# Filler matmuls, exponential buffers, halves of the softmax and the order of projection's products in a fused attention and two-MLP kernel

## The chip, the cores and the metric

The kernel runs on one core of a Trainium2 chip. The metric is the device time of one execution in microseconds; the time of a kernel is the median of its runs. TensorE (PE in the profile) multiplies and writes only into PSUM, which has eight banks here of 128 partitions by 512 float32 words; VectorE (DVE), ScalarE (ACT) and GpSimd (POOL) do the elementwise work, and SyncE (SP) issues most of the DMAs.

## The reference

Attention over 32 memory slots, then two MLPs, all in float32. B is 4, H 8, S 576, D 64, M 32; there are 2304 tokens, and the model is 512 wide.

```python
a = softmax(phi, axis=2)                       # over the 576 positions
k_m = einsum('bhsm,bhsd->bhmd', a, k)          # 32 memory rows per head
v_m = einsum('bhsm,bhsd->bhmd', a, v)
attn = softmax(q @ k_m.T / 8, axis=-1)         # over the 32 slots
x = (attn @ v_m) as (2304, 512)
x = ((x @ w_a) * (x @ w_b)) @ w_out            # 512 -> 1536 -> 512
h = x @ w_in                                   # 512 -> 2048
out = (h * sigmoid(1.702 h)) @ w_out2          # 2048 -> 512
```

The weights come as 64-bit floats and are decoded on the chip.

## The kernel before, in words

**The order is planned, not written.** Every piece of work is a Python generator, a stream with a priority, that yields requests: an engine with a cost in ns, a slot of a buffer, or a mark that another stream sets. `Order.run` (line 179) keeps one clock per engine, takes the request with the earliest start (in steps of 40 ns, then by priority, low numbers first) and lets that stream emit its instructions. So the order of the instructions on each engine's in-order queue comes from the planner's costs. A load sets its mark with the time at which it is taken to land, as soon as its DMA is issued in the plan (`load`, line 125; in the front 300 bytes per ns and 2500 ns to land, counted from 2000 ns); a stream that waits for that mark is resumed at once and uses the time as the earliest start of its next request.

**The front.** There are eight attention units, one for each batch and group of four heads: unit n is batch n // 2. `loads` (line 1626) issues the first loads in the order of the tuple `FIRST` (line 48): phi, k and v, and q of a unit, and raw weight pieces, each into a slot of its buffer; a load whose buffer isn't free holds up all behind it, on SyncE's queue too. Six raw buffers exist at first. `memory(n)` (line 524) takes a slot of `et_s`, the buffer of exponentials, then transposes phi on PE (line 551 in units 0 and 1, 548 later), takes maxima on DVE (555, 557), exponentials on ACT (561, 565), transposes back (569, 573), multiplies with k and v (589), and ends with the scores (628), which go transposed into `sT` (635). It holds two PSUM banks of `bank_a` meanwhile. `queries(n)` (499) transposes q (508). `softmax` (647) then runs over `sT`: for batch 0 in two halves of 288 positions, each a stream of its own, for the others whole. Its result is transposed by DVE into `aT` (675), one buffer for a unit, which both halves of a unit share and which is released when both are through, and is split into a high and a low part (`hi_lo`, 341: a copy on ACT at line 344 and a subtraction on DVE or POOL at line 338).

`decode_piece` (428) decodes a weight piece: two ACT passes (437, 441) and a DVE pass (443). Pieces 4 and up wait until attention of unit 1, first half, is there (`HOLDD`). Four decoded pieces and v_m give, by `fold` (774), the effective weights of a column group g and batch b: PE at line 795, ACT 813, DVE 815. `gated` (822) multiplies them with the attention of batch b, 48 matmuls of 288 columns at line 847 in two halves u, and stores the product of the two branches. Matmuls of this work use the PSUM banks of `bank_m`, two at first; `lend_banks` (687) moves two more over from the six of `bank_a`.

**Fillers.** `warm_up` (1577) has the last priority, 99. It takes a bank of `bank_m`, multiplies the identity with itself again and again, 300 ns by the planner's cost, and gives the bank back when the first gated product is stored.

**Projection.** After all gated products `project(p)` (990) runs for three groups of 768 tokens. It forms the second matmul of the first MLP by seven products of half-size blocks, as Strassen and Winograd do, in the order `STEPS` (1070), 36 matmuls of 384 columns each: two row blocks r inside three steps q. Several products add onto one chain of PSUM banks (`CHAINS`, 988): P1, P6, P7 and P4 on one, P5 and P3 on another, P2 on a third. What a chain holds between two of them is read first (`AFTER`, 989; `product_out`, 1027): ACT copies it after P1, P5 and P6, DVE adds it after P7, P3 and P2 (1050), ACT copies it after P4 (1054). `load_kept` (959) and `split_kept` (973) load and split the moving operands in the same order; `USED` says in which order the split weights lie, so that what the last group has used can be given away by its count.

The second MLP (lines 1284, 1485, 1516) follows and isn't touched.

Of the kernel before, what the change touches and what calls it, by code (L numbers as in the profile page):

```python
# [46 lines left out]

FIRST = (
    ("phi", 0), ("phi", 1), ("kv", 0), ("q", 0), ("kv", 1), ("q", 1), ("raw", 0), ("raw", 1), ("raw", 2), ("raw", 3),
    ("raw", 4), ("raw", 5), ("raw", 6), ("raw", 7), ("phi", 2), ("kv", 2), ("q", 2), ("phi", 3), ("kv", 3), ("q", 3),  # L50
    ("raw", 8), ("raw", 9), ("raw", 10), ("raw", 11), ("phi", 4), ("kv", 4), ("q", 4), ("phi", 5), ("kv", 5), ("q", 5),
)

# [142 lines left out]
def tile_mem_attention_moe_moe2(  # L196
# [109 lines left out]
    zero = pa.tile([P, 1], F32, name="zero")  # L306
    bdk = [pa.tile([P, HG * M], F32, name=f"bdk{i}") for i in range(2)]
    phi_s = slots(pa, 2, [P, HG, C0, M], "phi")
    et_s = slots(pa, 1, [P, C0, SP, 2], "et")
    kv_s = slots(pa, 2, [P, 2, HG, C0, D], "kv")  # L310
    q_s = slots(pa, 2, [P, QC, D], "q")
    mx_s = slots(pa, 3, [P, 6], "mx")
    kvn_s = slots(pa, 2, [P, 2, 2, D], "kvn")
    qT_s = slots(pa, 2, [P, HG, U], "qT")
    sT_s = slots(pa, 2, [P, S], "sT")
    aT_s = slots(pa, 1, [P, S], "aT")
    sm_s = slots(pa, 4, [P, S // M, 1], "sm")

    def attn(b, part, c, lo, n):
# [204 lines left out]
    def memory(n):  # L524
# [112 lines left out]
            ends.append(t1)  # L637
        parts = [(0, U), (U, U)] if b == 0 else [(0, S)]
        left = [len(parts)]
        place = []  # L640
        for i, (o, w) in enumerate(parts):
            od.spawn(
                (PA + PB * i) if b == 0 else 10 + n,
                softmax(ends[i] if b == 0 else max(ends), n, o, w, sT, place, left),
            )

    def softmax(t, n, o, w, sT, place, left):
        b, g = divmod(n, NHG)
        s2 = sT[0][:, o:o + w]
        s3 = s2.rearrange("p (s m) -> p s m", m=M)  # L650
        full = list(s3.shape)
        t, sm = yield DVE, t, dve(w), sm_s
        sm1 = sm[0][:, 0:w // M, :]
        nc.vector.reduce_max(out=sm1[:, :, 0], in_=s3, axis=AX.X)  # L654
        t = yield from combine(t, s3, s3, sm1.to_broadcast(full), ALU.subtract, w)
        t, _ = yield ACT, t, act(w)
        nc.scalar.activation(out=s3, in_=s3, func=AF.Exp, scale=scale)
        t, _ = yield DVE, t, dve(w)
        nc.vector.reduce_sum(out=sm1[:, :, 0], in_=s3, axis=AX.X)
        t, _ = yield DVE, t, 78  # L660
        nc.vector.tensor_scalar_add(sm1, sm1, 1e-9)
        t, _ = yield DVE, t, 125
        nc.vector.reciprocal(out=sm1, in_=sm1)
        t = yield from combine(t, s3, s3, sm1.to_broadcast(full), ALU.mult, w)
        sm_s.release(sm, t)
        if not place:

            place.append(None)
            place[0] = yield "slot", aT_s
            od.mark(place[0][1], "aT", n)  # L670
        t = max(t, (yield "mark", "aT", n))
        aT = place[0]
        a2 = aT[0][:, o:o + w]
        t, _ = yield DVE, max(t, aT[1]), dve(w)
        nc.vector.transpose(out=a2, in_=s2)
        left[0] -= 1
        if left[0] == 0:
            sT_s.release(sT, t)
        t = yield from hi_lo(t, attn(b, HI, g, o, w), attn(b, LO, g, o, w), a2, w)
        left.append(t)  # L680
        if len(left) == 1 + S // w:
            aT_s.release(aT, max(left[1:]))
        for e in range(2):
            if o <= e * U < o + w:
                od.mark(t, "attn", n, e)
# [273 lines left out]
    def load_kept():  # L959

        for p in range(NP):
            for name in STEPS:
                b = PRODUCTS[name][1]
                for q in range(NG1 // 2):
                    s = yield "slot", rg_s
                    t = s[1]
                    for i in range(p * N2 // U, ((p + 1) * N2 - 1) // U + 1):
                        for g in (2 * q, 2 * q + 1):
                            t = max(t, (yield "mark", "g1", g, i, (0, 0, 1, 2)[min(STORED[b], 3)]))
                    nc.sync.dma_start(out=s[0], in_=g1v[STORED[b], :, 2 * q:2 * q + 2, p * N2:(p + 1) * N2])  # L970
                    od.load(t, CW * N2 * 4, "rg", p, name, q)
                    loaded["rg", p, name, q] = s

    def split_kept():
        for p in range(NP):
            for name in STEPS:
                for q in range(NG1 // 2):
                    t = yield "mark", "rg", p, name, q
                    b = yield "slot", ring_s
                    od.spawn(PB1, split_one(max(t, b[1]), p, name, q, loaded.pop(("rg", p, name, q)), b))  # L980
# [9 lines left out]

    def project(p):
        held = {}
        for k, name in enumerate(STEPS):
            a, chain = PRODUCTS[name][0], CHAINS[name]
            first = (0, chain) not in held
            for q in range(NG1 // 2):
# [70 lines left out]
        "P1": (A11, B11), "P2": (A12, B21), "P3": (S4, B22), "P4": (A22, T4),  # L1067
        "P5": (S1, T1), "P6": (S2, T2), "P7": (S3, T3),
    }
    STEPS = ("P1", "P2", "P5", "P6", "P3", "P7", "P4")  # L1070
    USED = [PRODUCTS[x][0] for x in STEPS]
    NA = 4
    WK, WB = NA * 2 * NB, 7 * (NG1 - NA) * 2 * NB + 128
    STORED = {B11: 0, B21: 1, B22: 2, T1: 3, T4: 4, T3: 5, T2: 6}
# [56 lines left out]

    def room_kept():

        yield "mark", "b", NP - 1, STEPS[-1], NG1 // 2 - 1
        give(hb_s, views(acc, N2, 8, AN))
        for r in range(2):
            yield "mark", "yc", 1, r
# [438 lines left out]

    def warm_up():

        _, ps = yield PE, 0.0, 300, bank_m
        while ("g1", 0, 0, 1) not in od.marks:  # L1580
            nc.tensor.matmul(ps[0][:, :P], ident, ident, start=True, stop=True)  # L1581
            t, _ = yield PE, 0.0, 300
        nc.tensor.matmul(ps[0][:, :P], ident, ident, start=True, stop=True)
# [96 lines left out]
```

## Time and profile before

| | us |
|---|---|
| median of 3 runs | 752.06 (751.93 to 752.6) |
| profiled execution, whole | 752.25 |
| profiled execution, its span | 750.5 |
| TensorE busy | 738.3 |
| VectorE busy | 535.2 |
| ScalarE busy | 431.0 |
| GpSimd busy | 384.8 |

The span runs from the first to the last instruction of the profiled execution; the rest of its time lies around it. Times in the rows are from the span's start. PEld is TensorE's weight load, which runs beside its matmuls. A busy TensorE counts fillers as work. A matmul in float32 is recorded twice, a transpose once.

### The profile page before, as it was taken

How to read it: one execution, taken by the hardware profiler on the slowest of the kernel's cores; microseconds unless marked ns; L12 is line 12 of the kernel's file. 1: busy time of each engine (PE TensorE's matmuls, PEld its weight loads, DVE VectorE, ACT ScalarE, POOL GpSimd, SP SyncE). 2: the span in 40 equal slices, each digit the busy share in tenths (PEclk: the TensorE clock that was granted, in tenths of full speed). 3: DMA queues.
4: the chain of work that ended last, by engine and by line, in shares of the span. 5: the costliest groups of instructions: out<-in, count | busy, mean ns of one | idle time of the engine just before them, and what ended most of it. 6: DMA issues, size and time to landing. Idle time of an engine off the chain costs nothing.

```text
span 750.5 us, 14537 instructions
## 1 busy us (share of the span) xinstructions
PE 738.3 (98%) x5362; PEld 686.6 (91%) x5362; DVE 535.2 (71%) x798; ACT 431.0 (57%) x843; POOL 384.8 (51%) x346
## 2 busy tenths in 40 slices
PE   8999999999999999999989999999999999999997
PEld 8787778888889999899989999999998888999997
DVE  2868796558985546955899676666765697898884
ACT  2776764668773346546856655655665655444441
POOL 0415465537996605813999522333150296776661
PEclk9999999999999999999999999999999999999999
DMA  8899964687868876576624665444698944644411
GB/s 263 284 319 294 300 201 143 213 279 258 270 211 258 282 224 181 163 206 180 194 69 149 233 217 162 144 151 156 197 350 302 364 146 120 218 142 142 137 28 33
DMA packets 110359, 153.53 MB, mean 205 GB/s; under 512 B 8400, under 2 KB 89040, under 8 KB 110288
## 3 DMA queue, kind: packets, MB, share of 16 engines
q1 hardware_dynamic: 104928, 143.13, 59.8%
q10 hardware_dynamic: 5360, 9.47, 3.7%
q8 instruction: 42, 0.69, 0.4%
q14 instruction: 29, 0.24, 0.1%
HBM read 100.01 MB, written 52.56 MB: 203 GB/s over the span
## 4 chain that ended last, share of the span: by engine, by line
PE 93%; DVE 4%; ACT 1%; issue 1%; DMA 1%; POOL 0%; ACTq 0%; DVEq 0%; POOLq 0%
PE bank L1284 23%; PE bank L847 19%; PE bank L1009 15%; PE bank L1516 13%; PE bank L1485 12%; PE bank L795 3%; PE bank L1581 3%; DVE attn L338 1%; PE bank L589 1%; PE bank L508 1%; DMA raw<-in_moe_w_in_dram 1%; PE bank L628 1%; DVE acc L338 0%; PE bank L569 0%; PE bank L548 0%
## 5 line engine op out<-in xcount | busy, mean ns | idle before, releaser
L847 PEld LDWEIGHTS bank<-attn,eff 128*128 128x128 f32 x1152 | 154.5, 188 | 15.9 <-issue 5.5
L847 PE MATMUL bank<-attn,eff 128*128 128x288 f32 x1152 | 164.5, 298 | 1.0 <-DVE eff L815 0.9
L338 POOL TENSOR_TENSOR acc<-acc 128x512 f32<-128x512 f32 (+2 forms) x62 | 90.4, 1479 | 67.6 <-DVE w L338 27.6
L1326 DVE TENSOR_TENSOR acc<-bank,acc 128x384 f32<-128x384 f32 x168 | 89.7, 554 | 46.4 <-PE bank L1284 39.7
L338 DVE TENSOR_TENSOR w<-acc,w 128x512 fp32r<-128x512 f32 (+2 forms) x99 | 103.1, 1068 | 19.1 <-ACT w L344 19.0
L344 ACT ACTIVATE w<-acc 128x512 fp32r<-128x512 f32 (+2 forms) x129 | 74.9, 590 | 62.9 <-PE bank L1516 39.6
L1009 PE MATMUL bank<-attn,w 128*128 128x384 f32 x504 | 91.5, 335 | 3.1 <-DVE acc L1050 2.2
L344 ACT ACTIVATE attn<-acc 128x768 fp32r<-128x768 f32 (+2 forms) x80 | 60.9, 769 | 53.6 <-PE bank L1009 42.1
L1009 PEld LDWEIGHTS bank<-attn,w 128*128 128x128 f32 x504 | 87.6, 188 | 4.0 <-ACT w L344 2.5
L338 DVE TENSOR_TENSOR attn<-acc,attn 128x768 fp32r<-128x768 f32 (+2 forms) x57 | 66.7, 1181 | 32.2 <-ACT attn L344 29.4
L1336 ACT ACTIVATE acc<-acc 128x384 f32<-128x384 f32 x96 | 49.3, 524 | 46.7 <-DVE acc L1326 45.7
L338 POOL TENSOR_TENSOR attn<-acc,attn 128x768 fp32r<-128x768 f32 (+2 forms) x23 | 37.2, 1628 | 50.3 <-ACT attn L344 50.3
L891 POOL TENSOR_TENSOR gr<-gr 128x288 f32<-128x288 f32 x48 | 46.9, 977 | 18.0 <-DMA g1d<-gr 10.1
L1284 PE MATMUL bank<-attn,w 128*128 128x384 f32 x288 | 55.1, 334 | 0.0
L338 POOL TENSOR_TENSOR w<-acc,w 128x256 fp32r<-128x256 f32 (+2 forms) x28 | 32.1, 1157 | 44.3 <-ACT w L344 44.3
L1284 PEld LDWEIGHTS bank<-attn,w 128*128 128x128 f32 x288 | 50.4, 188 | 0.0
L1009 PE MATMUL bank<-attn,w1b 128*128 128x384 f32 x252 | 47.4, 335 | 0.8 <-DVE attn L338 0.8
L338 POOL TENSOR_TENSOR sT<-sT,sm 128x576 f32<-128x576 f32 (+1 forms) x16 | 16.9, 1057 | 60.3 <-DVE sm L654 34.6
L1284 PE MATMUL bank<-w1b,w 128*128 128x384 f32 x224 | 46.2, 334 | 0.0
L338 POOL TENSOR_TENSOR w<-dm,w 128x256 fp32r<-128x256 f32 x27 | 24.3, 906 | 40.7 <-ACT w L344 40.7
L1009 PEld LDWEIGHTS bank<-attn,w1b 128*128 128x128 f32 x252 | 44.0, 188 | 1.2 <-DVE attn L338 1.1
L1284 PE MATMUL bank<-w 128*128 128x384 f32 x224 | 43.8, 334 | 0.0
(182 smaller groups left out, 1462.2 us busy)
## 6 DMA issues: line engine op xcount, KB each, us to landing
acc<-g1d SPq DMA_DIRECT2D x63, 384.0 KB, 3.8
g2d<-acc SPq DMA_DIRECT2D x96, 192.0 KB, 2.5
raw<-in_moe_w_out_dram SPq DMA_DIRECT2D x24, 512.0 KB, 4.6
acc<-g2d SPq DMA_DIRECT2D x10, 1024.0 KB, 7.8
raw<-in_moe_w_in_dram SPq DMA_DIRECT2D x16, 512.0 KB, 4.3
acc<-g2d SPq DMA_DIRECT2D x16, 512.0 KB, 5.8
g1d<-gr SPq DMA_DIRECT2D x12, 576.0 KB, 4.8
g1d<-acc SPq DMA_DIRECT2D x8, 576.0 KB, 5.0
```

Source lines behind the costliest of these rows:

```text
L338: (nc.gpsimd if e == POOL else nc.vector).tensor_tensor(out=dst, in0=in0, in1=in1, op=op)
L344: nc.scalar.activation(out=hi, in_=src, func=AF.Copy)
L795: nc.tensor.matmul(ps[c][0][row(h), :], bdv[b][half, h, :], wt["wab", g, h][0][half, :], start=True, stop=True)
L847: nc.tensor.matmul(dst[:, :U], e[:, c, sw, i * CW + j * P:i * CW + (j + 1) * P], attn(b, mv, c, u * U, U), start=(n == 0), stop=(n == 3 * ...
L891: nc.gpsimd.tensor_tensor(out=dst, in0=in0, in1=in1, op=ALU.subtract)
L1009: nc.tensor.matmul(ps[0][:, :N2], w1_of(a, g, sw)[:, r * P:(r + 1) * P], b[0][:, mv, i], start=(first and q == n == 0), stop=(q == NG1 // ...
L1284: nc.tensor.matmul(ps[0][:, :N2], w[:, sw, r, :], y[mv][r], start=(n == 0), stop=(n == 5))
L1326: nc.vector.tensor_tensor(out=s[0], in0=ps[0][:, :N2], in1=x[0], op=ALU.add)
L1336: nc.scalar.activation(out=c[0], in_=c[0], func=AF.Gelu_apprx_sigmoid)
L1485: nc.tensor.matmul(ps[i, s][0], b[0][:, sw, c - o, :], wo2[c][:, mv], start=(c == n == 0), stop=(c == 4 * K4 - 1 and n == 2),)
L1516: nc.tensor.matmul(ps[name][0][:, :NB], x[0][:, sw, c, :], moving(b, h // 2 + c, mv), start=(h == c == n == 0), stop=(h > 0 and c == K4 - ...
L1581: nc.tensor.matmul(ps[0][:, :P], ident, ident, start=True, stop=True)
```

## The change

The fillers get a fixed start of 18 at a cost of 220 ns, then a wait for the mark of phi of unit 0, and go on until the fourth weight piece is decoded rather than until the first gated product is stored. Raw pieces 6 and 7 move behind the loads of unit 2. Exponentials have two buffers. Batch 0's softmax ends in two half buffers, each taken and released by one half of a unit; when all four halves are through, the whole becomes the buffer of the other batches. The second and third token groups of projection run their products in another order, and the weights are laid out in that order.

```diff
--- before.py
+++ after.py
@@ -47,7 +47,7 @@
 
 FIRST = (
     ("phi", 0), ("phi", 1), ("kv", 0), ("q", 0), ("kv", 1), ("q", 1), ("raw", 0), ("raw", 1), ("raw", 2), ("raw", 3),
-    ("raw", 4), ("raw", 5), ("raw", 6), ("raw", 7), ("phi", 2), ("kv", 2), ("q", 2), ("phi", 3), ("kv", 3), ("q", 3),
+    ("raw", 4), ("raw", 5), ("phi", 2), ("kv", 2), ("q", 2), ("raw", 6), ("raw", 7), ("phi", 3), ("kv", 3), ("q", 3),
     ("raw", 8), ("raw", 9), ("raw", 10), ("raw", 11), ("phi", 4), ("kv", 4), ("q", 4), ("phi", 5), ("kv", 5), ("q", 5),
 )
 
@@ -306,14 +306,15 @@
     zero = pa.tile([P, 1], F32, name="zero")
     bdk = [pa.tile([P, HG * M], F32, name=f"bdk{i}") for i in range(2)]
     phi_s = slots(pa, 2, [P, HG, C0, M], "phi")
-    et_s = slots(pa, 1, [P, C0, SP, 2], "et")
+    et_s = slots(pa, 2, [P, C0, SP, 2], "et")
     kv_s = slots(pa, 2, [P, 2, HG, C0, D], "kv")
     q_s = slots(pa, 2, [P, QC, D], "q")
     mx_s = slots(pa, 3, [P, 6], "mx")
     kvn_s = slots(pa, 2, [P, 2, 2, D], "kvn")
     qT_s = slots(pa, 2, [P, HG, U], "qT")
     sT_s = slots(pa, 2, [P, S], "sT")
-    aT_s = slots(pa, 1, [P, S], "aT")
+    aT_m = pa.tile([P, S], F32, name="aT")
+    aT_s, ah_s, ah_done = Slots(), Slots([aT_m[:, :U], aT_m[:, U:]]), []
     sm_s = slots(pa, 4, [P, S // M, 1], "sm")
 
     def attn(b, part, c, lo, n):
@@ -637,14 +638,13 @@
             ends.append(t1)
         parts = [(0, U), (U, U)] if b == 0 else [(0, S)]
         left = [len(parts)]
-        place = []
         for i, (o, w) in enumerate(parts):
             od.spawn(
                 (PA + PB * i) if b == 0 else 10 + n,
-                softmax(ends[i] if b == 0 else max(ends), n, o, w, sT, place, left),
+                softmax(ends[i] if b == 0 else max(ends), n, o, w, sT, left),
             )
 
-    def softmax(t, n, o, w, sT, place, left):
+    def softmax(t, n, o, w, sT, left):
         b, g = divmod(n, NHG)
         s2 = sT[0][:, o:o + w]
         s3 = s2.rearrange("p (s m) -> p s m", m=M)
@@ -663,23 +663,20 @@
         nc.vector.reciprocal(out=sm1, in_=sm1)
         t = yield from combine(t, s3, s3, sm1.to_broadcast(full), ALU.mult, w)
         sm_s.release(sm, t)
-        if not place:
-
-            place.append(None)
-            place[0] = yield "slot", aT_s
-            od.mark(place[0][1], "aT", n)
-        t = max(t, (yield "mark", "aT", n))
-        aT = place[0]
-        a2 = aT[0][:, o:o + w]
+        room = ah_s if b == 0 else aT_s
+        aT = yield "slot", room
+        a2 = aT[0]
         t, _ = yield DVE, max(t, aT[1]), dve(w)
         nc.vector.transpose(out=a2, in_=s2)
         left[0] -= 1
         if left[0] == 0:
             sT_s.release(sT, t)
         t = yield from hi_lo(t, attn(b, HI, g, o, w), attn(b, LO, g, o, w), a2, w)
-        left.append(t)
-        if len(left) == 1 + S // w:
-            aT_s.release(aT, max(left[1:]))
+        room.release(aT, t)
+        if b == 0:
+            ah_done.append(t)
+            if len(ah_done) == 2 * NHG:
+                aT_s.release([aT_m, 0.0], max(ah_done))
         for e in range(2):
             if o <= e * U < o + w:
                 od.mark(t, "attn", n, e)
@@ -959,7 +956,7 @@
     def load_kept():
 
         for p in range(NP):
-            for name in STEPS:
+            for name in STEPS[p]:
                 b = PRODUCTS[name][1]
                 for q in range(NG1 // 2):
                     s = yield "slot", rg_s
@@ -973,7 +970,7 @@
 
     def split_kept():
         for p in range(NP):
-            for name in STEPS:
+            for name in STEPS[p]:
                 for q in range(NG1 // 2):
                     t = yield "mark", "rg", p, name, q
                     b = yield "slot", ring_s
@@ -990,7 +987,7 @@
 
     def project(p):
         held = {}
-        for k, name in enumerate(STEPS):
+        for k, name in enumerate(STEPS[p]):
             a, chain = PRODUCTS[name][0], CHAINS[name]
             first = (0, chain) not in held
             for q in range(NG1 // 2):
@@ -1067,8 +1064,8 @@
         "P1": (A11, B11), "P2": (A12, B21), "P3": (S4, B22), "P4": (A22, T4),
         "P5": (S1, T1), "P6": (S2, T2), "P7": (S3, T3),
     }
-    STEPS = ("P1", "P2", "P5", "P6", "P3", "P7", "P4")
-    USED = [PRODUCTS[x][0] for x in STEPS]
+    STEPS = [("P1", "P2", "P5", "P6", "P3", "P7", "P4")] + (NP - 1) * [("P1", "P5", "P6", "P2", "P7", "P3", "P4")]
+    USED = [PRODUCTS[x][0] for x in STEPS[-1]]
     NA = 4
     WK, WB = NA * 2 * NB, 7 * (NG1 - NA) * 2 * NB + 128
     STORED = {B11: 0, B21: 1, B22: 2, T1: 3, T4: 4, T3: 5, T2: 6}
@@ -1131,7 +1128,7 @@
 
     def room_kept():
 
-        yield "mark", "b", NP - 1, STEPS[-1], NG1 // 2 - 1
+        yield "mark", "b", NP - 1, STEPS[-1][-1], NG1 // 2 - 1
         give(hb_s, views(acc, N2, 8, AN))
         for r in range(2):
             yield "mark", "yc", 1, r
@@ -1576,8 +1573,12 @@
 
     def warm_up():
 
-        _, ps = yield PE, 0.0, 300, bank_m
-        while ("g1", 0, 0, 1) not in od.marks:
+        _, ps = yield PE, 0.0, 220, bank_m
+        for _ in range(18):
+            nc.tensor.matmul(ps[0][:, :P], ident, ident, start=True, stop=True)
+            yield PE, 0.0, 220
+        yield "mark", "phi", 0
+        while ("wab", 0, 2 * NHG - 1) not in od.marks:
             nc.tensor.matmul(ps[0][:, :P], ident, ident, start=True, stop=True)
             t, _ = yield PE, 0.0, 300
         nc.tensor.matmul(ps[0][:, :P], ident, ident, start=True, stop=True)
```

## Rows read from the trace of the kernel before

**Rows 1.** Windows: us, busy us by engine, granted clock, DMA share, GB/s.

```profile
35.30:117.20 81.90, 79.91 (x906) 64.91 (x905) 61.27 (x135) 56.46 (x135) 38.14 (x39) 1.00 0.84 274
117.20:247.40 130.20, 130.10 (x1089) 114.70 (x1082) 91.37 (x124) 80.64 (x145) 87.33 (x81) 1.00 0.73 239
...
291.10:336.50 45.40, 43.76 (x249) 42.75 (x248) 35.13 (x32) 25.91 (x42) 28.14 (x17) 1.00 0.63 180
336.50:383.50 47.00, 44.75 (x258) 44.46 (x258) 35.46 (x34) 30.07 (x54) 33.02 (x27) 1.00 0.54 155
```

**Rows 2.** Timeline of PE in the front: start, us, instruction, records.

```profile
1.36 7.55 PE L1581 MATMUL bank<-ident 128*128 128x128 f32 x40 [1.36 <-POOL ident masks.py:199]
8.84 1.30 PE L551 MATMUL bank<-ident,phi 128*32 128x128 f32 x40
10.07 1.83 PE L1581 MATMUL bank<-ident 128*128 128x128 f32 x14
...
14.62 1.30 PE L551 MATMUL bank<-ident,phi 128*32 128x128 f32 x40
...
30.01 1.68 PE L795 MATMUL bank<-acc,gr 64*32 64x512 f32 x8
...
32.03 1.06 PE L795 MATMUL bank<-acc,gr 64*32 64x512 f32 x8
33.02 2.50 PE L1581 MATMUL bank<-ident 128*128 128x128 f32 x20
35.28 4.20 PE L847 MATMUL bank<-attn,eff 128*128 128x288 f32 x30
```

**Rows 3.** Timeline of the front: ACT, DVE and POOL.

```profile
17.20 0.69 ACT L561 ACTIVATE et<-bank,mx 128x512 f32<-128x512 f32 x1
...
23.42 0.67 ACT L437 ACTIVATE acc<-raw 128x512 f32<-128x512 f32 x1
...
29.89 0.69 DVE L443 SCALAR_TENSOR_TENSOR acc<-acc,raw_p 128x512 uint32<-128x512 uint32 x1
...
31.35 0.47 DVE L675 STREAM_TRANSPOSE aT<-sT 128x288 f32<-128x288 f32 x1
...
32.83 0.42 DVE L675 STREAM_TRANSPOSE aT<-sT 128x288 f32<-128x288 f32 x1
33.17 1.31 DVE L815 TENSOR_TENSOR eff<-bank,eff 128x512 fp32r<-128x512 f32 x2
...
34.17 0.80 POOL L338 TENSOR_TENSOR attn<-aT,attn 128x288 fp32r<-128x288 f32 x1 [0.44 <-ACT attn L344]
```

**Rows 4.** Timeline of SyncE's queue: issues of DMAs.

```profile
1.85 0.62 SPq L354 DMA_DIRECT2D phi<-in_phi_dram  x1
...
21.12 0.33 SPq L371 DMA_DIRECT2D raw_p<-in_moe_w_b_dram  x1
...
26.03 0.33 SPq L371 DMA_DIRECT2D raw<-in_moe_w_a_dram  x1
...
27.72 0.33 SPq L371 DMA_DIRECT2D raw<-in_moe_w_a_dram  x1
...
29.27 0.64 SPq L353 DMA_DIRECT2D phi<-in_phi_dram  x1
```

**Rows 5.** DMA issues of the first 6 us: KB, us from issue to landing.

```profile
phi<-in_phi_dram SPq DMA_DIRECT2D x1, 128.0 KB, 4.3
phi<-in_phi_dram ACTq DMA_DIRECT2D x1, 128.0 KB, 5.2
```

**Rows 6.** Windows, line 1581 alone: us, busy PE and PEld, clock, DMA.

```profile
2.50:3.50 1.00, 1.00 (x7) 1.00 (x6) 1.00 0.73 193
...
25.60:30.00 4.40, 4.40 (x38) 4.28 (x38) 1.00 0.59 185
```

**Rows 7.** PE's waits over the span: us in total, times, longest.

```profile
PE bank L1009 <- DVE acc L1050: 2.2, 1, 2.2
...
PE bank L1009 <- DVE attn L338: 1.4, 2, 0.8
```

## Prediction, made before the changed kernel was built or run

> **What bounds the kernel now.** I read the page's busy shares first, then the windows over the kernel's stages, then PE's waits, and last the timelines of the front and of projection. TensorE is the busiest engine throughout. By stage [rows 1] it is idle for 2.0 us between 35.3 and 117.2 (81.90 less 79.91), 0.1 us in the dense gated stage behind it, 1.6 us in projection's second group of tokens (45.40 less 43.76) and 2.2 us in its third (47.00 less 44.75). So from the first gated matmul at 35.28 on, some 6 us in all can be had by removing waits, and whatever starts that matmul earlier moves all that follows.
>
> But a busy TensorE is not a useful one. Up to 35.3 much of its time goes to filler matmuls (line 1581): 40 records at the start, 14 from 10.07, 20 more from 33.02 up to the first gated matmul [rows 2]. A float32 matmul leaves two records, so 40 are 20 fillers. The front is a chain through the attention units 0 and 1 (the first two passes of `memory`, `queries` and `softmax`), through the decoding of the first four weight pieces and through the first fold. It ends with two things that the gated matmul needs: effective weights, whose last subtraction runs 33.17 to 34.48, and attention of unit 1, first half, whose low part POOL makes 34.17 to 34.97 [rows 3]. The fillers hold the gated matmul back by no more than 0.3 us beyond these; the chain is what counts.
>
> **The fillers at the start.** The planner takes phi of unit 0 as due at 2000 + 294912/300 + 2500 = 5483 ns. With fillers at 300 ns it fits 19 ahead, and one more gets between the two parts of the transposes: 20, as the 40 records say. In the new text 19 steps cost 220 ns, so the planner is at 4180 when it goes on; the wait for the mark of phi does not stop it, since that mark is set when the load is planned, and its time is thrown away. Five more fit at 300 ns, so 24 fillers stand ahead of phi, four more than before. Phi's second DMA is issued at 1.85 and lands 4.3 us later [rows 4, 5], so phi is there at 6.2 to 6.8 while its transposes start at 8.84: the fillers already delay them. Four fillers are 8 records; at the pace of 25.6 to 30.0, 38 records in 4.40 us [rows 6], they cost 0.9 us. Bounds: nothing, if phi lands later than this, and 1.3 us at the pace of 2.5 to 3.5, 7 records in a microsecond.
>
> **Two buffers for exponentials.** `memory` takes its buffer before its first transposes, so with one buffer the planner couldn't place unit 1's transposes until unit 0's exponentials were used up: they run at 14.62, and 14 filler records stand where they could have been [rows 2]. Its phi is issued on ACT's queue in the same two microseconds and takes 5.2 us [rows 5], so it is there at about 7.2. With two buffers both units' transposes stand together: with the 0.9 us, 9.8 to 12.1. VectorE's maxima of unit 1 follow at 12.1 to 13.2, its exponential at about 13.5, instead of 17.20 [rows 3]: 3.7 us earlier. ACT and VectorE have the room there. The cost is that two units hold PSUM banks at once; that is a rival.
>
> **Softmax in halves.** With one buffer for a whole unit, both halves of unit 0 had to be through before unit 1 could write. The transposes come 1.5 us apart on VectorE, at 31.35 and 32.83 [rows 3], and unit 1's first half had its turn only behind unit 0's second. With a slot per half it can go ahead of it: 1.5 us on this branch. It adds no instruction and no bytes. Later batches get the whole buffer when all four halves are done, which is what they waited for before. On the attention branch 3.7 + 1.5 = 5.2 us.
>
> **The branch of decode and fold.** It must come forward as well. The four decodes run on ACT from 23.42, the last VectorE step ends at 30.58, and the fold's two parts stand at 30.01 and 32.03 [rows 2, 3]. The second part waits for a bank while the filler holds one of two; the filler's bank is now free at the fourth decode, which takes away up to 1.0 us. The rest comes with the order: unit 1's exponentials and copies leave ACT's and VectorE's queues ahead of the decodes, by some 3 us. No row shows how far the planner uses that. Bounds for the first gated matmul: 0, if the decodes stay where they are, and 5.2, if they follow attention. I take 4.0 us, nearer the upper end, as the decodes stand behind unit 1's work in both queues.
>
> **Loads.** SyncE issues raw piece 5 at 21.12 and piece 7 only at 27.72, since pieces 6 and 7 wait for buffers that the decodes free; phi of unit 2 stands behind them and goes at 29.27 [rows 4]. Moved past, phi, kv and q of unit 2 can go at about 21.5, 7.8 us earlier, and their 6.2 us of issues end about 27.7, while piece 6 went at 26.03: 1.7 us later for one piece, less for the next. These two are needed for the second fold, which also waits for pieces 4 and 5, held until attention of unit 1 is there. I put this at nothing: bounds a gain of the 2.0 us idle in the mixed stage and a loss of 1.7.
>
> **Projection.** PE's longest wait, 2.2 us, is product P4 of the third token group: it adds onto the chain that P7 leaves, and VectorE must read P7 first (line 1050) [rows 7]. P7 stands directly before P4, so the only cover is P7's second row block, 6 matmuls. In the new order P3 is between them: 36 matmuls, 6.2 us at the second group's 43.76 us for 252 [rows 1]. VectorE was late by 2.2, so this wait goes, and no other pair comes closer: P1 and P6, P6 and P7, P5 and P3 each keep a product between. The second group's wait of 1.4 us is for splits of the operands on VectorE [rows 7]. P2's additions (line 1050) stand between them in VectorE's in-order queue and wait for P2 to end; the new order takes them two products later. Bounds 0 and 1.6; I take half, 0.8. The rearranged weights are the same bytes, and the room freed in the last group depends on the count of products, not on their names.
>
> **Sum.** 4.0 + 2.2 + 0.8 = 7.0 us. The profiled execution took 752.25, with a span of 750.5; that gives 745.2. The median, 752.06, stands 0.2 lower, so the forecast is 745.1.
>
> **A rule that speaks against it.** With the fillers gone between fourth decode and first gated matmul, TensorE has little to do for some 3 us. In this trace it was never granted less than full speed: the stage windows read 1.00 [rows 1], also where it idled. The Trainium skill (TensorE: Matmul & The Clock Gate, "What's actually happening") says that the throttled clock is the default and activity releases it. By it the first gated step, 48 matmuls at 4.20 us for 30 [rows 2], could run at 1.2 GHz and take twice as long: an estimate of 6.7 us given back, hence 751.8. No row of this trace shows that level.
>
> **The rivals.**
> *Only projection counts.* The front's gain is lost in the mixed stage, because decodes and loads set its pace there and a TensorE that starts earlier waits more. For it: ACT and VectorE are 69% and 75% busy there [rows 1]. Against: the loads come earlier too, and the dense stage behind has no idle. Then 752.1 less 3.0 = 749.1. Chance 0.22.
> *Two units hold the banks.* After two of six attention banks are lent to the gated work, four are left; two units of `memory` with two banks each take all, and queries and scores wait, with TensorE's in-order queue behind them. The price: six units pass between 35 and 117; at 0.8 us each, PE's longest single wait for a split [rows 7], 4.8, and twice that, 9.6, if queries and scores both wait. It decides from 8.5 us on (7.0 + 1.5), so only in the second case: 745.1 + 9.6 = 754.7. Against: gated matmuls stand in the same queue and use other banks. Chance 0.07.
> *The clock falls.* The filler records show a slower pace, 7 in a microsecond against 38 in 4.40 [rows 6], 1.23 times as long or more, though the granted clock reads full. If the gated matmuls ran so until attention's end, from 31 to 64 (two fifths of the mixed stage), 0.23 of 33 us, 7.6, would be lost: 752.7, no change. Chance 0.03 for this or more.
> *It does not do what it says.* If the decodes stay where they are and VectorE is late elsewhere in projection, nothing is left: 751 to 753. Chance 0.05.
>
> **How the numbers follow.** The forecast has 0.63, its own range being 741 to 748 by the bounds of the front (0 to 5.2), the mixed stage (minus 2.0 to plus 1.7) and the splits (0 to 1.6). A measurement of this kernel can tell about 0.2%, 1.5 us, from no change. Faster by more: the forecast and nearly all of the first rival, 0.84. Within it: 0.08. Slower: the banks and a little of the clock, 0.08. The range 740.5 to 751.0 leaves out less than 2 in 10.
>
> **What would show it.** Right: 48 filler records ahead of line 551, then 80 records of line 551 together; unit 1's exponential at 13 to 14; first gated matmul at 30 to 32; phi of unit 2 issued at 21 to 22; no wait of TensorE for line 1050. Wrong: a first gated matmul after 34; idle TensorE of over 4 us between it and the dense stage; waits for PSUM reads by lines 331 or 635; a granted clock below 1.00 ahead of the gated matmuls.

## The result, and the profile after

The changed kernel takes 744.58 us (median of 4 runs, 744.49 to 747.05) against 752.24 for the kernel before: a ratio of 0.9906, 95% interval 0.9893 to 0.9919, or 7.7 us less. The forecast was 745.1. The profiled execution took 744.51 with a span of 742.7, 7.8 less than before.

The stages of that span, by the starts of the first gated matmul, of projection and of the second MLP, show where it came from:

| | before | after | change |
|---|---|---|---|
| start to first gated matmul | 35.28 | 33.33 | -1.95 |
| from there to projection | 212.07 | 208.76 | -3.31 |
| projection | 136.18 | 133.70 | -2.48 |
| second MLP to the end | 367.0 | 366.9 | -0.1 |

So the total was met, but not by the terms forecast (4.0, 0 and 3.0), and up to 1.4 of the first 1.95 isn't the change's (last section). Windows of the changed kernel over the stages of [rows 1], moved to its own times (the first one from its first gated matmul on); columns as there:

```profile
33.30:111.30 78.00, 75.78 (x884) 63.88 (x882) 62.95 (x143) 56.19 (x134) 31.86 (x35) 1.00 0.84 276
111.30:242.10 130.80, 130.80 (x1105) 114.82 (x1098) 91.82 (x124) 82.01 (x147) 92.28 (x85) 1.00 0.73 237
285.80:329.00 43.20, 42.76 (x242) 41.54 (x242) 34.44 (x28) 24.73 (x42) 31.71 (x20) 1.00 0.64 182
329.00:375.80 46.80, 46.26 (x266) 45.55 (x265) 33.54 (x33) 32.09 (x57) 31.47 (x25) 1.00 0.57 171
```

The mixed stage is 3.9 us shorter than in [rows 1] with as much recorded idle time (2.2 us). Its end isn't at quite the same work: it holds 22 matmul records fewer, and the dense stage, 0.6 longer, 16 more. So the 3.31 of the table is the figure to compare. Projection's second and third groups have 0.4 and 0.5 us of idle time left, where they had 1.6 and 2.2.

Timeline of PE in the front after the change; lines have moved (fillers 1578 and 1582, phi's transposes 552, scores 629, first fold 792, phi's copy transposed 549, gated 844):

```profile
1.36 5.77 PE L1578 MATMUL bank<-ident 128*128 128x128 f32 x36 [1.36 <-POOL ident masks.py:199]
6.96 1.50 PE L1582 MATMUL bank<-ident 128*128 128x128 f32 x12
8.40 1.30 PE L552 MATMUL bank<-ident,phi 128*32 128x128 f32 x40
...
10.05 1.30 PE L552 MATMUL bank<-ident,phi 128*32 128x128 f32 x40
...
23.91 0.71 PE L629 MATMUL bank<-qT,bdk 64*32 64x288 f32 x16
...
28.77 1.05 PE L792 MATMUL bank<-acc,gr 64*32 64x512 f32 x6
30.05 1.07 PE L792 MATMUL bank<-acc,gr 64*32 64x512 f32 x10 [0.23 <-DVE acc L444]
32.81 0.76 PE L549 MATMUL bank<-ident,et 128*128 128x128 f32 x5 [1.69 <-POOL et L540]
33.33 3.40 PE L844 MATMUL bank<-attn,eff 128*128 128x288 f32 x24
```

The 48 filler records ahead of phi are there, and the second unit's transposes follow the first's with one filler between. The branches on ACT, DVE and POOL, same stretch:

```profile
12.78 0.68 ACT L562 ACTIVATE et<-bank,mx 128x512 f32<-128x512 f32 x1
...
23.16 0.68 ACT L438 ACTIVATE acc<-raw 128x512 f32<-128x512 f32 x1
...
29.30 0.69 DVE L444 SCALAR_TENSOR_TENSOR acc<-acc,raw_p 128x512 uint32<-128x512 uint32 x1
...
31.60 0.48 DVE L670 STREAM_TRANSPOSE aT<-sT 128x288 f32<-128x288 f32 x1
32.00 1.25 DVE L812 TENSOR_TENSOR eff<-bank,eff 128x512 fp32r<-128x512 f32 x2
...
32.72 0.80 POOL L339 TENSOR_TENSOR attn<-aT,attn 128x288 fp32r<-128x288 f32 x1
```

Unit 1's exponential stands at 12.78 instead of 17.20 [rows 3], but the decodes begin 0.3 us earlier only and end 0.6 earlier. SyncE's queue:

```profile
21.64 0.64 SPq L354 DMA_DIRECT2D phi<-in_phi_dram  x1
...
28.64 0.53 SPq L372 DMA_DIRECT2D raw<-in_moe_w_a_dram  x1
```

Phi of unit 2 goes 7.6 us earlier than in [rows 4], raw piece 6 2.6 us later. The waits of PE that answer to [rows 7]:

```profile
PE bank L549 <- POOL et L540: 1.7, 1, 1.7
...
PE bank L1006 <- DVE attn L339: 0.9, 3, 0.5
```

The wait for P7's addition is gone, that for splits is down from 1.4 to 0.9, and a new wait for POOL's copy of phi stands ahead of the first gated matmul.

### The profile page after: what moved, and what is told of

Read it like the earlier page. It is cut to its first block, busy times and chain, and to the rows that moved or that the text cites. A ratio compares the mean times of both kernels' runs of the same rounds, so it can differ in the third digit from the quotient of the medians.

```text
span 742.7 us, 14507 instructions
## 1 busy us (share of the span) xinstructions
PE 732.1 (99%) x5344; PEld 682.7 (92%) x5344; DVE 533.2 (72%) x799; ACT 430.8 (58%) x842; POOL 386.1 (52%) x347
## 4 chain that ended last, share of the span: by engine, by line
PE 92%; DMA 3%; POOL 2%; DVE 2%; SPq 1%; issue 0%; ACT 0%; DVEq 0%; POOLq 0%
PE bank L1281 24%; PE bank L844 21%; PE bank L1006 16%; PE bank L1513 14%; PE bank L1482 12%; PE bank L792 3%; DMA q<-in_q_dram 1%; PE bank L590 1%; DMA raw_p<-in_moe_w_b_dram 1%; DMA kv<-in_k_dram 1%; PE bank L509 1%; POOL w L339 1%; SPq L372 1%; POOL attn L339 1%; DVE attn L339 0%
## 5 line engine op out<-in xcount | busy, mean ns | idle before, releaser
L339 POOL TENSOR_TENSOR acc<-acc 128x512 f32<-128x512 f32 (+2 forms) x65 | 95.0, 1481 | 68.2 <-DVE w L339 27.9
L339 DVE TENSOR_TENSOR w<-acc,w 128x512 fp32r<-128x512 f32 (+2 forms) x100 | 105.0, 1076 | 20.5 <-ACT w L345 20.4
L339 POOL TENSOR_TENSOR attn<-acc,attn 128x768 fp32r<-128x768 f32 (+2 forms) x26 | 41.9, 1623 | 35.8 <-ACT attn L345 35.8
L888 POOL TENSOR_TENSOR gr<-gr 128x288 f32<-128x288 f32 x48 | 44.6, 931 | 17.0 <-issue 7.0
L339 POOL TENSOR_TENSOR w<-acc,w 128x256 fp32r<-128x256 f32 (+2 forms) x27 | 30.0, 1119 | 44.4 <-ACT w L345 44.3
L339 POOL TENSOR_TENSOR sT<-sT,sm 128x576 f32<-128x576 f32 (+1 forms) x12 | 13.5, 1126 | 64.0 <-DVE sm L654 31.7
```

Of the source, the lines that this page charges most:

```text
L339: (nc.gpsimd if e == POOL else nc.vector).tensor_tensor(out=dst, in0=in0, in1=in1, op=op)
L888: nc.gpsimd.tensor_tensor(out=dst, in0=in0, in1=in1, op=ALU.subtract)
```

## Experiments

Every kernel was profiled and timed beside the kernel before on its chip; ratios are to that. One table holds the stages of all the profiled executions, in us, read as above:

| kernel | median | ratio, 95% interval | first gated | to projection | projection |
|---|---|---|---|---|---|
| before | 752.24 | | 35.3 | 212.1 | 136.2 |
| changed | 744.58 | 0.9906 (0.9893, 0.9919) | 33.3 | 208.8 | 133.7 |
| s_alone | 751.44 | 0.9988 (0.9979, 0.9996) | 33.9 | 212.1 | 136.4 |
| no_f | 752.01 | 0.9992 (0.9980, 1.0003) | 32.9 | 216.6 | 133.7 |
| no_e | 758.72 | 1.0086 (1.0073, 1.0100) | 34.4 | 219.1 | 136.1 |
| no_h | 756.18 | 1.0048 (1.0035, 1.0061) | 32.8 | 218.7 | 136.3 |
| no_s | 749.19 | 0.9953 (0.9939, 0.9967) | 33.6 | 208.8 | 135.5 |
| skip_12 | 743.38 | 0.9878 (0.9865, 0.9891) | 32.1 | 209.6 | 133.7 |
| pa_222 | 756.04 | 1.0052 (1.0032, 1.0072) | 33.6 | 219.0 | 135.9 |
| pa_230 | 754.09 | 1.0021 (1.0013, 1.0030) | 33.0 | 215.6 | 136.3 |
| pa_240 | 747.86 | 0.9936 (0.9917, 0.9956) | 32.7 | 211.7 | 134.0 |
| pb_290 | 760.03 | 1.0089 (1.0058, 1.0119) | 35.3 | 218.7 | 137.3 |
| pb_305 | 761.35 | 1.0104 (1.0068, 1.0139) | 36.1 | 220.1 | 136.8 |
| pb_310 | 758.64 | 1.0076 (1.0063, 1.0089) | 35.6 | 216.2 | 136.3 |

The first gated matmul isn't always the start of steady gated work: no_f, no_h, pa_222 and pa_230 run one to three of them, wait, and go on at 33.86, 35.51, 35.06 and 33.78.

### One part alone, and one part undone

**s_alone**, on the kernel before; the loops over `STEPS` then read `STEPS[p]`, as in the change:

```diff
-    STEPS = ("P1", "P2", "P5", "P6", "P3", "P7", "P4")
-    USED = [PRODUCTS[x][0] for x in STEPS]
+    STEPS = [("P1", "P2", "P5", "P6", "P3", "P7", "P4")] + (NP - 1) * [("P1", "P5", "P6", "P2", "P7", "P3", "P4")]
+    USED = [PRODUCTS[x][0] for x in STEPS[-1]]
```

> The kernel before with projection's order of products alone changed. Theory: in the changed kernel projection and what leads up to it took 2.5 us less (383.53 less 247.35 before, 375.79 less 242.09 after), and that belongs to the order alone: 749.7 (749.2 to 750.2), no wait of TensorE for line 1050. Rival: the waits shrank because the front's shift moved other work away from them: 751.5 to 752.5, with a wait for splits in place of that for P7's addition.

Measured: 751.44, 0.9 us less than its neighbour. The theory fell; the rival holds by its mechanism, just below its range. PE's waits in this kernel:

```profile
PE bank L1009 <- POOL attn L338: 2.5, 3, 1.1
...
PE bank L1009 <- DVE attn L338: 1.4, 2, 0.8
```

The wait for line 1050 is gone, as it should; the 2.2 us come back as waits for operand splits that the planner now gives to POOL (0.2 in the kernel before). Projection is no shorter (136.4). The first gated matmul at 33.9 with the same work up to there is no gain of the order; it is the start of TensorE, told in the last section.

**no_f**, on the changed kernel:

```diff
-    ("raw", 4), ("raw", 5), ("phi", 2), ("kv", 2), ("q", 2), ("raw", 6), ("raw", 7), ("phi", 3), ("kv", 3), ("q", 3),
+    ("raw", 4), ("raw", 5), ("raw", 6), ("raw", 7), ("phi", 2), ("kv", 2), ("q", 2), ("phi", 3), ("kv", 3), ("q", 3),
```

> The changed kernel with the loads of unit 2 behind raw pieces 6 and 7 again. Theory: the mixed stage's gain of some 4 us comes from unit 2's loads being issued 7.6 us earlier, so it goes: 748 to 749, first gated matmul still near 33.3, dense stage beginning near 115. Rival: the second buffer for exponentials and the half buffers make that gain, so little changes: 744.5 to 745.5.

**no_e**, on the changed kernel:

```diff
-    et_s = slots(pa, 2, [P, C0, SP, 2], "et")
+    et_s = slots(pa, 1, [P, C0, SP, 2], "et")
```

> The changed kernel with one buffer for exponentials. Theory: loads set the front's pace, and unit 1's exponential being 4.4 us earlier moved its scores by 1.0 us only, so the first gated matmul goes back by 1 us or less; 745 to 746. Rival: the second buffer also lets later units overlap and makes the mixed stage's gain of 4 us: 748 to 749.

**no_h**, on the changed kernel: `softmax` and the buffer `aT` as before.

```diff
-    aT_m = pa.tile([P, S], F32, name="aT")
-    aT_s, ah_s, ah_done = Slots(), Slots([aT_m[:, :U], aT_m[:, U:]]), []
+    aT_s = slots(pa, 1, [P, S], "aT")
```

> The changed kernel with batch 0's softmax in one whole buffer again. Theory: unit 1's first half waits for unit 0's second again, but the effective weights end last by then, so the first gated matmul goes back by less than 1 us: 744.6 to 745.6. Rival: it was the 1.5 us of the prediction: 746 or more, first gated matmul at 34.8.

Measured: 752.01, 758.72 and 756.18. Each part, undone by itself, costs 7 to 14 us, as much as the whole change brings or twice that. No theory had such numbers; of the rivals only that of no_h, 746 or more, covers its time, and its sign, a first gated matmul at 34.8, did not come (32.8). Parts whose losses sum to 33 us can't each be worth their loss in a gain of 7.7. The first gated matmul moves by 1.1 us at most (32.8 to 34.4); most of the loss, 7.9, 10.4 and 9.9 us, lies between it and projection, and projection itself is 2.4 and 2.7 longer in no_e and no_h. Between them two things show, here in no_e. TensorE's and VectorE's timelines, and below them the windows of all engines (PE, PEld, DVE, ACT, POOL):

```profile
60.62 1.05 PE L792 MATMUL bank<-acc,gr 64*32 64x512 f32 x4
...
62.36 2.50 DVE L444 SCALAR_TENSOR_TENSOR acc<-acc,raw_p 128x512 uint32<-128x512 uint32 x2
...
63.72 3.11 PE L792 MATMUL bank<-acc,gr 64*32 64x512 f32 x4 [2.05 <-DVE acc L444]
...
64.92 0.18 PEld L792 LDWEIGHTS bank<-acc,gr 64*32 64x32 f32 x2 [1.02 <-DVE acc L444]
...
66.77 1.11 PE L570 MATMUL bank<-ident,et 128*128 128x128 f32 x4
```

```profile
60.00:62.00 2.00, 1.63 (x8) 0.56 (x8) 2.00 (x5) 1.08 (x2) 0.79 (x1) 1.00 0.90 254
62.00:64.00 2.00, 0.28 (x1) 0.18 (x2) 2.00 (x4) 1.46 (x5) 1.92 (x3) 0.75 1.07 393
64.00:66.00 2.00, 2.00 (x4) 0.18 (x2) 1.93 (x4) 0.67 (x3) 1.44 (x2) 0.50 0.96 287
...
72.00:74.00 2.00, 2.00 (x35) 1.62 (x25) 1.37 (x4) 1.16 (x2) 0.00 (x0) 0.69 0.03 8
```

A fold waits 2.05 us for a decoded piece, with all of TensorE's queue behind it. VectorE, busy without a pause from 60 to 64, decodes that piece behind other work and takes 1.25 us for each step, where it took 0.69 in the front. While TensorE idles the granted clock (the column ahead of the DMA share) falls to 0.50, 1.2 GHz, until about 73. Some 10 us at half speed cost about 5, by estimate. A wait of that length doesn't always bring a fall: 2.16 us for POOL's copy of phi, up to 33.88, left the clock of this kernel at 1.00. The other two kernels fall as well: no_h is at 0.50 from 35.4 to 38.8 and from 66 to 73, no_f from 34.2 to 37.7. Neither the kernel before nor the changed one falls ahead of its last microsecond.

In no_h the first fall stands in a wait for the very part that was undone:

```profile
34.51 0.47 DVE L675 STREAM_TRANSPOSE aT<-sT 128x288 f32<-128x288 f32 x1
...
35.51 2.93 PE L847 MATMUL bank<-attn,eff 128*128 128x288 f32 x9 [1.28 <-ACT attn L344]
```

The fourth gated matmul is the first that needs unit 1's attention. In the changed kernel it runs at once, behind the second of the four transposes of batch 0 (31.60); in no_h it waits for the third (34.51). So without the half buffers unit 1's first half does stand behind unit 0's second.

The Trainium skill (TensorE: Matmul & The Clock Gate, "What's actually happening") says that the throttled clock is the default and activity releases it; these runs agree, with 0.50 granted behind an idle queue. The prediction priced a slow first gated step at 6.7 us, for the changed kernel, where it did not come; in no_f and no_h, where the clock fell at that step, it stayed low for 3.4 us, half of which is 1.7.

### The order of products undone in the changed kernel, and fillers left out

**no_s**: as s_alone, the other way round.

```diff
-    STEPS = [("P1", "P2", "P5", "P6", "P3", "P7", "P4")] + (NP - 1) * [("P1", "P5", "P6", "P2", "P7", "P3", "P4")]
+    STEPS = NP * [("P1", "P2", "P5", "P6", "P3", "P7", "P4")]
```

> The changed kernel with projection's products in one order for all three token groups, as before; TensorE's instructions up to projection are the same. Theory: the order gives what projection shows, 136.1 us instead of 133.7: 747.0, with the 2.2 us wait for line 1050 back. Rival: as with the order alone on the kernel before, where projection took 136.5, it gives about 1 us or nothing: 744.5 to 745.5.

Measured: a profiled execution of 746.57, 2.1 us over that of the changed kernel, of which 0.3 stand ahead of the first gated matmul and 1.8 in projection; the wait is back:

```profile
PE bank L1006 <- DVE acc L1047: 2.3, 1, 2.3
```

The median of 749.19 is higher because the runs spread from 746.57, at a mean granted clock of 1.000, to 750.33, at 0.995, which this edit doesn't explain. With the clock near full, 746.57 and 746.68, theory and rival are told apart: behind this front the order is worth 1.8 us; s_alone showed that behind another it is worth 0.9 at most.

**skip_12**: the plan stays, and 12 of the 24 fillers ahead of phi are not emitted.

```diff
-        for _ in range(18):
-            nc.tensor.matmul(ps[0][:, :P], ident, ident, start=True, stop=True)
+        for i in range(18):
+            if i >= 12:
+                nc.tensor.matmul(ps[0][:, :P], ident, ident, start=True, stop=True)
             yield PE, 0.0, 220
```

> The changed kernel with the first 12 of the 24 fillers ahead of phi left out and the planned order of everything else kept. Theory: phi's transposes start when phi lands, near 6.5 instead of 8.4, but loads of q and of k and v set the pace from there on, so the first gated matmul stays within 0.5 us of 33.3: 744 to 745. Rival one: the fillers delay the chain by all of 1.9 us: 742.5. Rival two: with half the fillers TensorE's slow start lasts longer and the chain is no earlier: 745 to 748.

Measured: 743.38. PE's timeline in this kernel:

```profile
6.77 1.30 PE L552 MATMUL bank<-ident,phi 128*32 128x128 f32 x40
...
22.29 0.71 PE L629 MATMUL bank<-qT,bdk 64*32 64x288 f32 x16
...
27.15 1.28 PE L792 MATMUL bank<-acc,gr 64*32 64x512 f32 x6
...
32.11 3.41 PE L844 MATMUL bank<-attn,eff 128*128 128x288 f32 x24
```

Against the changed kernel phi's transposes, unit 1's scores and the first fold all stand 1.6 us earlier, the first gated matmul 1.2. So loads do not set the pace of this front, and my theory of it fell: the chain in TensorE's queue does, and fillers ahead of phi delay it in full. But projection begins 0.4 us earlier only (241.7): the rest is given back ahead of it. The profiled execution was 744.21 against 744.51. The two ratios' intervals miss each other by 0.0002; whether this kernel beats the changed one by the 1.2 us of the medians is not settled, since they were timed beside different runs of the kernel before.

### The same parts in another order

The losses above had a second reading. An edit that moves a planned time changes the order of hundreds of instructions behind it: in the traces of no_f, no_e, no_h and the six kernels below, some 300 to 700 of TensorE's 5350 matmul records stand in another order than in the kernel they were made from, in skip_12 none. These kernels keep every part of one side, and change one number that only the planner sees, the cost of a filler: pa_222, pa_230 and pa_240 on the changed kernel,

```diff
-            yield PE, 0.0, 220
+            yield PE, 0.0, 230
```

pb_290, pb_305 and pb_310 on the kernel before, where 300 becomes 290, 305 or 310. (A filler or two more or less follow from it.)

> The changed kernel with the planner's cost of the 18 first fillers at 230 ns instead of 220: every part of the change is there, and the planner's order of the work comes out another. Theory: the parts make the gain, each by its own effect: 743.5 to 746.5. Rival: the gain needs just this order, since undoing any one part lost 7 to 14 us, more than all of the gain: 748 to 758.

> The kernel before with the planner's cost of its fillers at 310 ns instead of 300: another order, no part of the change. Theory (parts make the gain): 751 to 753.5. Rival (any new order moves the time by several us, either way): outside 750 to 755.

> The changed kernel with the first 18 fillers planned at 222 ns instead of 220. Theory: what the planner's order happens to be is worth several us either way, and 744.6 is a good one among the changed kernel's: 746 to 757. Rival: the order at 230 ns was an outlier and the parts give their gain here: 743.5 to 746.

> The changed kernel with the first 18 fillers planned at 240 ns. Theory as for 222 ns: 746 to 757. Rival: 743.5 to 746.

> The kernel before with fillers planned at 290 ns instead of 300. Theory: its 752 is a good order among its own too, so 753 to 762, and the means of both families, four orders each, lie 3 us or more apart in favour of the change only if the parts give something of their own. Rival: 751 to 753, the order at 310 ns being an outlier.

> The kernel before with fillers planned at 305 ns. Theory: 753 to 762. Rival: 751 to 753.

Measured, in the order of the numbers: 756.04, 754.09 and 747.86 on the changed side, 760.03, 761.35 and 758.64 on the other. For 230 and 310 the theory, that the parts alone make the gain, fell and the rival held; the other four met the theory that was then made of that rival. No order came to the 743.5 to 746 of the parts alone, and none of the other side came back to 751 to 753. Both 744.58 and 752.24 are the best of the four orders of their side. In pa_222 the clock falls twice; the windows of PE (the number ahead of the last two columns):

```profile
30.00:40.00 10.00, 7.80 (x46) 0.83 0.99 326
...
60.00:70.00 10.00, 8.36 (x65) 0.83 0.77 252
```

pb_290 and pb_305 have such falls between 65 and 76, pa_230 a short one from 64 to 68; pa_240 and pb_310 have none there. Of the six kernels that fall near 65, five do so in a fold's wait for a decoded piece (0.8 to 2.6 us) or within 1.6 us behind it, and no_h behind a wait for ACT's copy of q. Near 35 no_f and pa_222 fall behind waits for effective weights.

pb_290 and pb_305 fall a third time, from 383 and 385 on, in the very wait that the new order of products takes away:

```profile
383.55 5.83 PE L1009 MATMUL bank<-attn,w 128*128 128x384 f32 x24 [2.24 <-DVE acc L1050]
```

```profile
384.00:386.00 2.00, 2.00 (x8) 2.00 (x8) 2.00 (x2) 0.00 (x0) 2.00 (x2) 0.50 0.00 0
```

The clock was low for 3.4 us, about 1.7 lost, on top of the 2.2 us of the wait. In the kernel before, pb_310 and no_s the same wait left it at 1.00.

The falls are not all of it. Half of the time at 0.50 is 1.7 to 6.8 us in the seven kernels with falls, which lie 7.4 to 14.1 above the best of their side; outside pb_290 and pb_305 it is less than half of that. And pb_305 took 758.00 in a run with a mean granted clock of 1.000.

The means say, roughly, what the parts are worth apart from the order: 758.1 for the four orders before (752.24, 760.03, 761.35, 758.64) and 750.6 for the four changed ones, 7.4 us. By the scatter of the eight (standard deviations 4.1 and 5.3) that difference is uncertain by 3.3 (one standard error), so an effect of the parts is likely but no more than roughly sized. Without the best of each side, the three other orders have means of 760.0 and 752.7, 7.3 apart, and don't overlap. By stage, from the table: the first gated matmul comes 2.4 us earlier on average (35.6 and 33.2), and each of the four changed orders is earlier than each of the four others, though pa_222 goes on only at 35.06; projection is 1.7 us shorter (136.7 and 135.0), in two of four by more than 2 and in two hardly; the stage between is 3.0 us shorter (216.8 and 213.8), with a range of 8 us on one side and 10 on the other.

## Why the prediction was right, and where it was not

**The fillers at the start.** Right in count (48 records), and skip_12 shows that they cost what they take. The 0.9 us for four more does not show against the kernel before, whose phi's transposes start at 8.84, since TensorE's slow start was shorter in this execution (last section). Against s_alone, with the old fillers and nearly the same slow start, it does:

```profile
7.44 1.30 PE L551 MATMUL bank<-ident,phi 128*32 128x128 f32 x40
```

8.40 is 0.96 later. The slow pace was misread: the 7 records of [rows 6] are those that reach into the microsecond, and they start 0.213 us apart against 0.112 at the fast pace, which is 1.9 times and not 1.23. So the upper bound of four fillers was 1.7 us, not 1.3, and the rival of the clock used too small a ratio.

**Two buffers for exponentials.** Unit 1's exponential came 4.4 us earlier where 3.7 was forecast. The step that failed is the next one, that the chain behind it follows: unit 1's scores came 1.0 us earlier, 24.92 to 23.91 (the former from the same view of the kernel before), because unit 1's products with k and v (19.50, before 21.00) stand behind unit 0's scores in TensorE's queue, and these hardly moved (18.85, before 18.98).

**Softmax in halves.** The mechanism was right, as no_h shows: unit 1's first half is transposed second (31.60) instead of third (32.83), and the third now comes 1.57 us behind it. But POOL's low part, the last of the attention branch, ends at 33.52 instead of 34.97, 1.45 earlier in all where 5.2 was forecast.

**Decode and fold.** The term of 4.0 us was mis-sized: 1.95 measured, 2.4 as a mean over orders. Against s_alone (33.87), whose slow start was as short, it is 0.5; the kernel before lost 1.41 us at this place by a slow start 2.94 us longer than that of s_alone, and with all eight put to one slow start at this rate the mean over orders is 2.1, by estimate. It rested on "some 3 us" for the decodes, and they moved by 0.3 to 0.6; the effective weights then set the start (33.25). The lower bound was for this case.

**The mixed stage.** Forecast at nothing with a gain of at most 2.0, the recorded idle time; measured 3.3. The bound was wrong. A busy TensorE in the record isn't one at its pace, as the weight loads show: they were busy for 64.91 of 81.90 us in the mixed stage and 114.70 of 130.20 in the dense one [rows 1]; at the dense stage's share the same loads take 73.7, so 8.2 us could be had, not 2.0. (An estimate: it takes the two stages' mixes of matmuls as alike.) The Trainium skill (Trainium Kernel Development and Optimization, "Performance Expectations") says that matmul busy time judges badly how close a kernel is to its limit and the weight loads' share judges well; the trace agrees: after the change that share is 82% (63.88 of 78.00) instead of 79%, while the matmuls' own stayed at 97 to 98%.

What made the stage shorter is shown in small part. Some 0.7 of the 3.3 us is work that left the stretch: unit 2's five transposes (32.81, before at 39.32; 0.5) now stand ahead of the first gated matmul, and so does the last filler (0.2). The mechanism of the loads is plain in the DMAs. The stretch in which SyncE waited for raw buffers, first before, then after (PE's windows, DMA share and GB/s last):

```profile
26.00:28.00 2.00, 2.00 (x20) 1.00 0.49 141
```

```profile
26.00:28.00 2.00, 2.00 (x20) 1.00 1.03 348
```

and the bytes of the first 60 us, before and after:

```profile
DMA packets 13287, 17.47 MB, mean 291 GB/s; under 512 B 1228, under 2 KB 9567, under 8 KB 13279
```

```profile
DMA packets 14505, 18.53 MB, mean 309 GB/s; under 512 B 1298, under 2 KB 10785, under 8 KB 14497
```

In all six kernels with the old load order these are 17.3 to 17.7 MB, in seven of the eight with the new one 18.1 to 18.5 (no_h has 17.7). Phi of unit 2 is issued at 28.0 to 29.5 in the six and at 21.6 to 24.2 in the eight. That the units' inputs are asked for earlier is thus an effect of the load order, whatever the plan. (Raw piece 6 went 2.6 us later, where 1.7 was forecast.) That the 3.3 us come from it is not shown: pa_222 moved 18.20 MB and lost 10 us in this stage.

**Projection.** 3.0 forecast, 2.5 measured. The wait for P7's addition went in every kernel with the new order, as argued. The step that holds only sometimes is that nothing takes its place: in five of nine kernels with the new order waits for splits on POOL do, 2.5 us in s_alone, and projection takes 135.9 to 136.4. The term also left out what the wait for P7 can cost beside its 2.2 us: the clock fell in it in pb_290 and pb_305. The 0.8 us for splits in the second group was measured as 1.2 less idle time there (1.64 and 0.44), with 0.5 back in the third.

**The rivals.** The clock did not fall in the changed kernel's profile ahead of its last microsecond; that it falls in its neighbours makes 0.03 a low price for that rival. Starved PSUM banks show, but in small:

```profile
62.25 0.33 PE L509 MATMUL bank<-ident,q 128*128 128x128 f32 x1 [1.18 <-ACT qT L330]
```

The transpose of q waits until ACT's copy frees a bank; 0.2 us more is a wait for VectorE's branch of that copy (line 332, 331 before), one of the signs named as wrong. 1.4 us in all are far from the 4.8 and 9.6 of that rival, and it isn't the second buffer alone: pb_310, with one, waits 2.1 us at the same place.

The forecast was right in sum because the mixed stage gave what the front did not, and that is luck: the terms were 2.0 and 0.5 too high and 3.3 too low, and of the three other orders with the same parts only one (747.86) lies in the forecast's own 741 to 748. What stays open is what makes the other 2.6 us of the mixed stage, and why one order has no long idle stretch near 35 and 65 and another has. The waits that end last there are named above; why the planner's order leads to them was read for no_e and no_h only.

## What to carry to other kernels

Where a planner makes the order, undoing one part measures a new order along with the part: leave the plan alone and drop instructions, as in skip_12, or perturb a number without meaning and compare means over several orders. A wait that goes in one queue is a gain only if the next producer isn't as late. Judge the room in a TensorE-bound stage by its weight loads and by the work done, not by the idle time between records, and look at the granted clock of any stretch in which its queue runs dry.

## What the runs showed of the hardware that was not expected

TensorE's slow start is not in the granted clock of the rows, and its length differs between executions. The fillers of the kernel before and of s_alone are the same instructions; PE's windows of the two, in that order:

```profile
5.00:6.00 1.00, 1.00 (x7) 1.00 0.83 188
```

```profile
5.00:6.00 1.00, 1.00 (x11) 1.00 0.81 189
```

Both read 1.00, but 7 filler records reach into the one microsecond and 11 into the other. In the kernel before the 1.00 was not measured there: the traces' record of the granted clock begins, with 1.00, at 7.30 us in the kernel before and at 4.36 in s_alone, and the views print 1.00 where they have no entry. At just that time fillers that started 0.213 us apart start 0.112 apart, in these two and in every other profile but skip_12, whose fillers end there. That is nearly twice the pace, as between the two levels of the clock (1.2 and 2.4 GHz). The time of it lies between 4.4 and 7.3 us in the 14 profiles, and all of the front follows: 33.9 and 35.3 for the first gated matmul. Of the 2.0 us that the front seemed to gain, up to 1.4 is this. So the granted clock of [rows 6], 2.50 to 3.50, is no sign of full speed.

A low clock can stand beside a PE that is recorded as busy: in no_e it is at 0.50 from 64 on, with four matmuls filling the two microseconds to 66 (the windows shown above), where the idle stretch ahead of it was 2.05 us. The weight loads tell it better: 0.18 of the 2.00 us, with 1.02 idle until the second decoded piece. So TensorE mostly waited there.
